# Steps of the last two block inverses put sooner in their slots, and the last output product split by columns, in an RWKV-7 chunk kernel with a SoLU layer

## The chip, the cores and the metric

The kernel runs on one core of one Trainium2 chip. The metric is device time in microseconds of one execution, as the median of several runs. One execution was also recorded by the hardware profiler; its times are given in microseconds from the start of its span.

TensorE is PE in the profile (PEld is its weight load), VectorE is DVE, ScalarE is ACT, GpSimd is POOL, SyncE is SP. A "q" behind a name (ACTq, SPq) means the issue of a transfer by that engine's queue.

## The reference

Two blocks follow one another, all in float32. The first is a recurrence with a decaying state for each of 4 batches and 8 heads (sequence 768, head size 40); the second is a layer with a SoLU activation and a layer norm on the 3072 tokens of 320 numbers that the first gives.

```python
for t in range(S):                                   # per batch and head, state is 40 x 40
    y[t]  = r[t] @ state
    Sa    = state @ a[t]
    state = state * w[t][None, :] - outer(Sa, b[t]) + outer(v[t], k[t])
x = y rearranged to (3072, 320)
h = x @ w_in                                         # 320 -> 1024
sm = exp(h - max(h)) / sum(exp(h - max(h)))
solu = h * sm
ln = (solu - mean(solu)) / sqrt(var(solu) + 1e-6) * g_ln
out = ln @ w_out                                     # 1024 -> 320
```

## The kernel before

The sequence is cut in chunks of 64 tokens. A unit of work, here called chunk i, is one such piece for a pair of batches with all 8 heads; there are N = 24 of them, two pairs of batches in turn, so chunks i and i + 2 belong to the same sequence. Inside a chunk the recurrence is written as matrix products, which need the inverse of a triangular 64 x 64 matrix for each head and batch. That inverse is put together from 32 x 32 blocks.

**The inverses.** The blocks of two chunks (GRP = 2) are inverted together by `invert`, a Python generator. VectorE works them out column by column: a *step* is one pair of instructions, a product (`prod`, L428) and a subtraction from `uu` (L430), and there are 30 steps for an inverse. All steps of one inverse depend on one another. The blocks come in by transfers issued on POOL (`blk<-nt_dram`, L412), from the matrices `nt` that earlier chunks wrote to memory (L401). With the last step two transfers are issued on SP (L436) that write the result to `uu_dram`; `bring` later reads it into `tu` and `uh` (L449, L451, also on SP). There are 12 inverses; the last two are numbered 10 (chunks 20 and 21) and 11 (chunks 22 and 23).

**The order of work.** All engines follow the order in which the program is written (`manual_schedule`). The main loop runs over i from -1 to 27 as a software pipeline: iteration i prepares chunk i + 5 (`front`, `norm`, AHEAD = 5), scores chunk i + 1, finishes the state of chunk i, and runs the second block for chunks i - 2 to i - 4 (`hidden`, `highest`, `exped`, `weighed`, `spreadof`, `folded`, `output`). Near the end the parts for chunks past 23 drop out. From i = 16 on there are no more loads of `w`; `norm` runs for the last time at i = 18 and `solved` at i = 23.

**The slots.** The steps of the inverse are dealt out by `some(n)` at four places of an iteration, called slots 0 to 3 here; how many a slot takes is in `shares`, or a default:

```python
pieces = shares.get(i, (0, 5, 4, 4) if i % GRP else (3, 5, 4, 5))
```

On VectorE the order within an iteration is: slot 0; the masks of `psi` and `lv` (L375) and the product `aT` (L366); slot 1; the *flip*, a 32 x 32 transpose of `tu` (L457); the row maximum `nmax` (L670); slot 2; the masks of `nt` and `lu` (L375); the product `e` (L684) and the statistics (L692 to L700); slot 3; the output `x` of the chunk (L619) and its state sum `tot` (L634). An inverse is begun in an even iteration, ahead of slot 3, but takes its first step only in the next iteration.

TensorE's order within an iteration is: `pu`, `ps`, `pst`, turned inputs `pa` and `pb`, two products into `h`, the first half of the output product `po`, `py` (which reads the flipped `tu`), `pnt`, `pl`, the second half of `po`, `pz`, `pyo` (which reads `lu`), `px`, more of `h` and `pyo`, the transposes `plnT`, then `pk`, `pv`, `pr`. The PSUM tiles `pu`, `ps`, `py`, `pnt`, `pl`, `pz`, `pyo` and `px` share two buffers (`ps1`, bufs = 2), so each waits until an earlier one has been read. While `norm` runs, `pz` takes over a buffer that the mask of `nt` reads, and `pyo` one that the mask of `lu` reads; from i = 19 on, without `pnt`, `pyo` still follows `lu`.

`xT` (L625, L626 on SP) takes `x` on to the second block; these transfers stand on SP ahead of the reads of the next iteration's `bring`.

**The output.** `output(i, 0)` does the first four of the eight products of chunk i with `w2` (width DM = 320) into one PSUM bank, `output(i, 1)` the last four; then ScalarE scales the bank into `osb` (L727) and issues its transfer to memory (L728). `osb` has a single buffer, so it can be written again only when the transfer before has ended. In the last iteration, i = 27, nothing but the output of chunk 23 is left. The lnT tile that it reads is copied by ScalarE in two halves (L713), four of the eight products from each.

Of the kernel before, what the change touches and what calls it, by code (L numbers as in the profile page):

```python
# [9 lines left out]
FP32 = mybir.dt.float32  # L10
# [3 lines left out]
AF = mybir.ActivationFunctionType  # L14
# [3 lines left out]
P = 128  # L18
C = 64
# [29 lines left out]
def kernel(  # L49
# [18 lines left out]
    nc = tc.nc  # L68
    B, H, S, D = r.shape
    DM = H * D  # L70
# [3 lines left out]
    N = NPAIR * NCH  # L74
    NF = DFF // P
# [5 lines left out]
    two = ctx.enter_context(tc.tile_pool(name="two", bufs=2))  # L81
# [14 lines left out]
    def c_(name):  # L96
        lo, hi = where[name]
        return cst[:, lo:hi]
# [20 lines left out]
    for x in ex_t:  # L119
# [10 lines left out]
                          in_=c_("eye_hi").unsqueeze(1).to_broadcast([P, 8, Q]))  # L130
    w_in = const.tile([P, 2 * NK - 1, DFF // 2], FP32, name="w_in")
    w2 = const.tile([P, NF, DM], FP32, name="w2")
# [6 lines left out]
    def bank(name):  # L139
        return ps3.tile([P, 512], FP32, tag="bank", name=name)  # L140
# [133 lines left out]
    def where_(i):  # L274
        return i % NPAIR, i // NPAIR
# [7 lines left out]
    def ok(i):  # L283
        return 0 <= i < N
# [430 lines left out]
    def output(i, x):  # L715
        if not ok(i):
            return
        d = st[i]
        bp, ci = where_(i)
        if x == 0:  # L720
            d["out"] = bank("po")
        for f in range(x * NF // 2, x * NF // 2 + NF // 2):
            nc.tensor.matmul(d["out"][:, 0:DM], lhsT=d["lnT"][:, f, :], rhs=w2[:, f, :], start=f == 0, stop=f == NF - 1)  # L723
        if x == 0:
            return
        osb = two.tile([P, DM], FP32, tag="osb", name="osb", bufs=1)
        nc.scalar.activation(out=osb, in_=d["out"][:, 0:DM], func=AF.Copy, scale=d["rs"])  # L727
        nc.scalar.dma_start(out=out.rearrange("(b s) n -> b s n", b=B)[2 * bp:2 * bp + 2, ci * C:ci * C + C], in_=osb)  # L728


    steps = []
# [79 lines left out]


    shares = {-1: (0, 2, 3, 9), 0: (4, 5, 3, 4), 1: (0, 6, 4, 5), 2: (4, 4, 3, 4), 3: (0, 5, 4, 4), 4: (6, 1, 4, 6)}
    narrowed = {-1: (0, 1, 0), 0: (0, 1, 1), 1: (1, 0, 2), 2: (0, 1, 2), 3: (1, 0, 1)}
    for i in range(-1, N + 3 + LAG):
        j, m = i + AHEAD, i - LAG
# [29 lines left out]
        left(i - 1)  # L846
        decay(j + 2)
        output(m - 3, 0)

        some(pieces[2])  # L850
# [12 lines left out]
        if i == 2 + LAG:  # L863
            mean = mean_of(4, 6, mean)
        output(m - 3, 1)

        close(i + 1)
# [48 lines left out]
```

## Time and profile before

| what | value |
|---|---|
| median of 3 runs | 621.12 us (618.76 to 623.91) |
| profiled execution, own time | 617.47 us |
| its span | 615.7 us |
| mean granted TensorE clock | 0.938 |
| TensorE busy | 547.3 us (89%) |
| VectorE busy | 448.7 us (73%) |
| ScalarE busy | 265.6 us (43%) |
| GpSimd busy | 257.7 us (42%) |
| start of `pu` in iterations 17, 18, 19, 20, 21 | 443.31, 464.27, 485.00, 505.16, 524.56 us |

A line of a timeline or group reads: start, length in us, engine, line of the program, operation, output <- inputs, partitions x elements, count, and in brackets how long the engine had stood still before it and what ended that. A line of the chain of waits has start, length and what ran; the chain is followed back from the last instruction to whatever released each one. The slices of the page cut the span in 40 equal parts, with the busy share in tenths (9 is 90% or more).

### The profile page before, as it was taken

Reading aid. Unit: us, or ns where it says so; the run is one execution under the profiler, and the core shown is the slowest. Engines: PE = TensorE matmul, PEld = TensorE weight load, DVE = VectorE, ACT = ScalarE, POOL = GpSimd, SP = SyncE. Lnnn points to the kernel's source line nnn. Section 1 sums busy time; section 2 is a strip of 40 time slices with the busy share of each in tenths; the row PEclk is TensorE's granted clock in tenths of the full one; section 3 lists DMA queues with packets and bytes.
Section 4 is the critical chain, followed back from the end, with each engine's and each line's share of the span. In section 5 each row is a group of like instructions: output and inputs, shape, how many; then the busy total and the mean of one; then the engine's idle time right before and its main releaser. Section 6 shows DMA issues by size and latency. Waiting matters only on the chain.

```text
span 615.7 us, 26656 instructions
## 1 busy us (share of the span) xinstructions
PE 547.3 (89%) x11453; PEld 397.4 (65%) x11453; DVE 448.7 (73%) x1262; ACT 265.6 (43%) x548; POOL 257.7 (42%) x424
## 2 busy tenths in 40 slices
PE   4555587689899999999999999999999999999994
PEld 3334476566576777777777677777777676676652
DVE  4797978979968869868868868688698688443431
ACT  4434455454443544454454445444433343342221
POOL 3462272472452472473365355534624631322200
PEclk9666767789999999999999999999999999999998
DMA  8986895664445454564565574564532612310100
GB/s 166 156 157 132 176 176 107 139 137 84 82 105 98 94 118 94 97 118 99 94 122 97 95 127 97 111 110 82 109 56 53 122 44 44 65 35 26 28 19 21
DMA packets 213901, 59.93 MB, mean 97 GB/s; under 512 B 199120, under 2 KB 208952, under 8 KB 213784
## 3 DMA queue, kind: packets, MB, share of 16 engines
q1 hardware_dynamic: 195512, 33.78, 32.5%
q0 software_dynamic: 11568, 19.78, 13.9%
q10 hardware_dynamic: 6704, 4.67, 2.7%
q8 instruction: 90, 1.47, 1.0%
q14 instruction: 27, 0.22, 0.1%
HBM read 40.10 MB, written 13.37 MB: 87 GB/s over the span
## 4 chain that ended last, share of the span: by engine, by line
PE 71%; DVE 15%; DMA 4%; issue 3%; ACT 3%; SPq 1%; POOL 1%; ACTq 0%; DVEq 0%; POOLq 0%
PE po L723 16%; PE h L257 15%; PE pyo L257 7%; DVE prod L428 4%; DVE uu L430 4%; PE pu L257 4%; PE plnT L712 4%; PE ps L257 3%; PE px L257 3%; PE py L257 2%; PE pl L257 2%; PE pz L257 2%; PE pst L505 2%; PE pr L342 1%; PE pei L342 1%
## 5 line engine op out<-in xcount | busy, mean ns | idle before, releaser
L257 PE MATMUL h<-w_in,xT 128*128 128x512 f32 (+1 forms) x288 | 123.0, 610 | 0.0
L723 PE MATMUL po<-w,lnT 128*128 128x320 f32 x384 | 112.7, 438 | 0.5 <-ACT lnT L713 0.5
L430 DVE TENSOR_TENSOR uu<-uu,prod 128x30 f32<-128x30 f32 (+4 forms) x360 | 102.1, 284 | 12.4
L428 DVE TENSOR_TENSOR prod<-blk,uu 128x30 f32<-128x30 f32 (+4 forms) x360 | 97.6, 271 | 9.6
L723 PEld LDWEIGHTS po<-w,lnT 128*128 128x128 f32 x384 | 71.0, 190 | 32.6 <-issue 4.1
L401 POOL DMA_DIRECT2D nt_dram<-nt x20 | 18.9, 943 | 120.0 <-DVE nt L375 98.5
L375 DVE TENSOR_TENSOR psi<-ps,cst 128x512 f32<-128x512 f32 x24 | 16.6, 690 | 66.6 <-PE ps L257 66.6
L701 POOL TENSOR_TENSOR rs<-c,mhalf 128x1 f32<-128x1 f32 x24 | 13.5, 561 | 112.1 <-DVE c L700 103.2
L650 POOL DMA_DIRECT2D xT<-x x96 | 48.7, 512 | 0.0
L257 PEld LDWEIGHTS h<-w_in,xT 128*128 128x128 f32 (+1 forms) x288 | 37.4, 189 | 9.2 <-issue 8.1
L670 DVE TENSOR_REDUCE nmax<-h 128x1 f32<-128x1024 f32 x24 | 28.6, 1193 | 18.6 <-PE h L257 18.6
L412 POOL DMA_DIRECT2D blk<-nt_dram x46 | 36.6, 802 | 10.8 <-issue 6.8
L257 PE MATMUL pyo<-lv,kb 64*64 64x104 f32 x768 | 37.8, 266 | 2.2
L257 PEld LDWEIGHTS pyo<-lv,kb 64*64 64x64 f32 x768 | 23.9, 140 | 20.9 <-issue 20.8
L638 POOL TENSOR_TENSOR st<-tot,ex 104x160 f32<-104x160 f32 x44 | 21.8, 512 | 36.6 <-DVE tot L634 23.5
L257 PE MATMUL pyo<-lu,kb 64*64 64x104 f32 x768 | 36.7, 258 | 0.0
L469 ACT ACTIVATE wy<-py,cst 128x256 f32<-128x256 f32 x24 | 11.4, 473 | 56.2 <-PE py L257 56.2
L280 POOL DMA_DIRECT2D raw_r<-in_r_dram x48 | 33.9, 709 | 0.0
L727 ACT ACTIVATE osb<-po,rs 128x320 f32<-128x320 f32 x24 | 12.7, 527 | 48.5 <-PE po L723 32.9
L554 ACT COPY x<-px 128x320 f32<-128x320 f32 x24 | 10.2, 425 | 54.1 <-PE px L257 54.0
L678 ACT ACTIVATE e<-h,nmax 128x1024 f32<-128x1024 f32 x24 | 26.6, 1108 | 14.3 <-DVE nmax L670 14.3
L684 DVE TENSOR_TENSOR e<-h,e 128x1024 f32<-128x1024 f32 x24 | 29.2, 1217 | 4.6 <-ACT e L678 4.6
(128 smaller groups left out, 1162.6 us busy)
## 6 DMA issues: line engine op xcount, KB each, us to landing
blk<-nt_dram POOLq DMA_DIRECT2D x46, 128.0 KB, 4.4
nt_dram<-nt POOLq DMA_DIRECT2D x20, 256.0 KB, 3.5
raw_w<-in_w_dram SPq DMA_DIRECT2D x48, 80.0 KB
a<-in_a_dram SPq DMA_DIRECT2D x48, 80.0 KB
raw_r<-in_r_dram POOLq DMA_DIRECT2D x48, 80.0 KB, 3.1
lv<-in_v_dram SPq DMA_DIRECT2D x48, 80.0 KB
out_dram<-osb ACTq DMA_DIRECT2D x24, 160.0 KB
raw_b<-in_b_dram SPq DMA_DIRECT2D x44, 80.0 KB
```

Source lines behind the costliest of these rows:

```text
L257: nc.tensor.matmul(o, lhsT=lhsT, rhs=rhs, start=start, stop=stop, skip_group_check=True)
L280: queue.dma_start(out=x[half(p), :, 0:D], in_=ap[2 * bp + p, :, ci * C:(ci + 1) * C, :].rearrange("h t d -> t h d"))
L412: queue.dma_start(out=nb[home:home + Q], in_=blocks[n][:, Q * e:Q * e + Q, Q * e:Q * e + Q])
L428: nc.vector.tensor_tensor(out=t, in0=nb[:, j:j + 1, j + 1:Q].to_broadcast([P, n_c, m]), in1=u[:, 0:n_c, j:j + 1].to_broadcast([P, n_c, m]) ...
L430: nc.vector.tensor_tensor(out=u[:, 0:n_c, j + 1:Q], in0=u[:, 0:n_c, j + 1:Q], in1=t, op=ALU.subtract)
L638: nc.gpsimd.tensor_tensor(out=to3(old), in0=to3(tot[0:W2]), in1=ex[:, :, 2 * q:2 * q + 2, C:].to_broadcast([W2, 2, 2, D]), op=ALU.mult)
L650: nc.gpsimd.dma_start(out=xT[to:to + Q, 2], in_=x[at + P - 3 * D:at + D, 2])
L670: nc.vector.tensor_reduce(out=nmax, in_=d["h"], axis=AX.X, op=ALU.max, negate=True)
L678: nc.scalar.activation(out=e, in_=d["h"], func=AF.Exp, bias=d["nmax"], accum_out=d["esum"])
L684: nc.vector.tensor_tensor(out=d["e"], in0=d["h"], in1=d["e"], op=ALU.mult)
L712: nc.tensor.transpose(out=t[:, j * P:(j + 1) * P], in_=d["e"][:, f * P:(f + 1) * P], identity=ident)
L723: nc.tensor.matmul(d["out"][:, 0:DM], lhsT=d["lnT"][:, f, :], rhs=w2[:, f, :], start=f == 0, stop=f == NF - 1)
```

## The change

Two edits. The first gives iterations 17 to 20 their own entries in `shares`, so that the 30 steps of inverse 10 (iterations 17 and 18) and of inverse 11 (19 and 20) are dealt out in other slots. The counts before, by the default, are 0,5,4,4 in 17 and 19 and 3,5,4,5 in 18 and 20. The entries of 18 and 20 add up to more than is left of the inverse; what is left is taken, so slot 3 of iteration 18 and slots 2 and 3 of iteration 20 stay empty, and slot 1 of iteration 20 takes five.

The second concerns chunk 23 alone. Its `output(23, 0)` issues nothing, and `output(23, 1)` makes all eight products for the left 160 columns, scales and sends them, and then the same for the right 160 columns in another PSUM bank. The two halves of `osb` are written and sent separately.

```diff
+        to = out.rearrange("(b s) n -> b s n", b=B)[2 * bp:2 * bp + 2, ci * C:ci * C + C]
+        osb = two.tile([P, DM], FP32, tag="osb", name="osb", bufs=1) if x else None
+
+        if i == N - 1:
+            for lo in (0, DM // 2) if x else ():
+                part = slice(lo, lo + DM // 2)
+                t = d["out"] if lo == 0 else bank("po")
+                for f in range(NF):
+                    nc.tensor.matmul(t[:, part], lhsT=d["lnT"][:, f, :], rhs=w2[:, f, part], start=f == 0, stop=f == NF - 1)
+                nc.scalar.activation(out=osb[:, part], in_=t[:, part], func=AF.Copy, scale=d["rs"])
+                nc.scalar.dma_start(out=to[:, :, part], in_=osb[:, part])
+            return
...
-        osb = two.tile([P, DM], FP32, tag="osb", name="osb", bufs=1)
         nc.scalar.activation(out=osb, in_=d["out"][:, 0:DM], func=AF.Copy, scale=d["rs"])
-        nc.scalar.dma_start(out=out.rearrange("(b s) n -> b s n", b=B)[2 * bp:2 * bp + 2, ci * C:ci * C + C], in_=osb)
+        nc.scalar.dma_start(out=to, in_=osb)
...
     shares = {-1: (0, 2, 3, 9), 0: (4, 5, 3, 4), 1: (0, 6, 4, 5), 2: (4, 4, 3, 4), 3: (0, 5, 4, 4), 4: (6, 1, 4, 6)}
+    shares.update({17: (0, 6, 5, 6), 18: (5, 6, 2, 4), 19: (0, 7, 6, 6), 20: (6, 6, 4, 4)})
```

## The prediction

> **What bounds the kernel now.** I read the page's busy line and slices first, then the chain that ended last, then the timelines of TensorE and VectorE through iterations 17 to 20 (443 to 524 us, the only ones whose step counts change), then the end. Lines from all of them, in that order:
>
> ```profile
> PE 547.3 (89%) x11453; PEld 397.4 (65%) x11453; DVE 448.7 (73%) x1262; ACT 265.6 (43%) x548; POOL 257.7 (42%) x424
> PE   4555587689899999999999999999999999999994
> DVE  4797978979968869868868868688698688443431
> ...
> 487.93 4.10 DMA tu<-uu_dram
> 492.12 0.46 DVE tu L457
> 492.71 0.67 PE py L257 x32
> ...
> 471.76 0.67 PE L257 MATMUL py<-tu,nt 64*64 64x32 f32 x32
> 492.71 0.67 PE L257 MATMUL py<-tu,nt 64*64 64x32 f32 x32 [1.18 <-DVE tu L457]
> 496.64 0.67 PE L257 MATMUL pyo<-rT,s 40*64 40x64 f32 x32
> 512.13 0.67 PE L257 MATMUL py<-tu,nt 64*64 64x32 f32 x32 [0.43 <-DVE tu L457]
> ...
> 466.43 0.69 DVE L375 TENSOR_TENSOR psi<-ps,cst 128x512 f32<-128x512 f32 x1 [2.35 <-PE ps L257]
> 471.26 0.44 DVE L457 STREAM_TRANSPOSE tu<-tu 128x256 f32<-128x256 f32 x1
> 492.12 0.45 DVE L457 STREAM_TRANSPOSE tu<-tu 128x256 f32<-128x256 f32 x1 [0.79 <-DMA tu<-uu_dram]
> 495.78 0.68 DVE L375 TENSOR_TENSOR lu<-pl,cst 128x512 f32<-128x512 f32 x1
> 511.55 0.44 DVE L457 STREAM_TRANSPOSE tu<-tu 128x256 f32<-128x256 f32 x1
> ...
> 608.31 0.53 ACT L727 ACTIVATE osb<-po,rs 128x320 f32<-128x320 f32 x1 [4.23 <-PE po L723]
> 608.87 0.53 ACTq L728 DMA_DIRECT2D out_dram<-osb  x1
> ...
> DMA  0000001111110111110111111111100000000001
> GB/s 0 0 0 0 0 15 29 15 44 59 15 51 7 51 37 37 37 15 37 44 59 44 44 59 44 59 44 44 51 0 0 0 0 0 0 0 0 0 0 47
> ```
>
> TensorE is full (9 in every slice from the middle to the last) and mostly hands over to itself. In the four iterations it stands still for only 1.18 and 0.43 us, both times ahead of `py`, for the flip (L457). The first of these waits has a transfer behind it: the tenth inverse's write (5.29 us in the chain) and read (4.10 us). VectorE is not the bound by its sum, but two things in its queue release TensorE in every iteration: the flip, which `py` waits for, and the masks at L375, which free the PSUM buffers of `pz` and `pyo`. At iteration 18 the flip ends (471.26 + 0.44 = 471.70) just as TensorE arrives; at 19 the mask of `lu` ends at 496.46 and `pyo` starts at 496.64. There is next to no slack in front of either. The last two lines are 609 to 616 us in 0.175 us slices: the last output drains from 609.9 to 614.0 us at a tenth of the DMA engines.
>
> [...] The output is 2 x 64 x 320, [...] with a busy share of 0.13 to 0.14 (2 of 16 is 0.125). [...] Here a 1.7 us wait of `pk` for `lnT` leaves it at 1.00; this decides a rival below.
>
> **The change, first part: the steps.** It adds and removes no step. One step is a pair L428, L430 of 0.45 to 0.65 us from start to start (447.82 to 448.27 for the first; 458.71 to 459.34 for the eleventh). An iteration has four slots: 0 ahead of the masks of `psi`, 1 ahead of the flip, 2 ahead of the masks of `nt` and `lu`, 3 ahead of `x`. Counts before are 0,5,4,4 / 3,5,4,5 / 0,5,4,4 / 3,5,4,5 for iterations 17 to 20. After, they are 0,6,5,6 / 5,6,2,0 / 0,7,6,6 / 6,5,0,0, since each inverse has 30. So every flip gets more steps in front of it. I carry the delay S of TensorE through, with 0.58 us from a flip's start to `py` (492.12 to 492.71; 511.55 to 512.13) and 0.14 us from a mask's end to the matmul.
>
> Iteration 17. Slot 1 has one step more (0.52): flip at 450.67, `py` at 451.25 for 451.09. Slot 2 then holds steps 7 to 11, 2.9 us for 2.2: mask of `nt` from 455.04 to 455.72, of `lu` to 456.32. `pz` wants the buffer of `nt` and `pyo` that of `lu`; `pyo` starts at 456.46 for 455.82. S = 0.64. Slot 3 is six steps, 4.1 us; `x` and `tot` end near 464.7, before `ps` (465.23 + 0.64) needs their buffer.
>
> Iteration 18. Slot 0, five steps, 3.06 us: 464.64 to 467.70, while `psi` could start at 466.43 + 0.64 = 467.07. The masks and `aT` take 1.81, slot 1 is six steps, 3.06: flip at 472.57, `py` at 473.15 for 471.76. S = 1.39. Slots 2 and 3 are nearly empty, and VectorE catches up; nothing on TensorE waits for that.
>
> Iteration 19. The tenth inverse is done before 475.1 instead of 481.5; its last step issues the two `uu_dram` writes on SP, which stands idle there (its next are the `xT` transfers), so they hold up nobody, and its read, behind the four `xT` transfers on SP, lands near 490.2, and the transfer no longer holds the flip. But `psi` starts at 487.16 + 1.39 = 488.55, the new inverse's steps at 490.31, and seven of them are 3.42: flip at 493.73, `py` at 494.31 for 492.71. The wait of 1.18 us is not gained: what is late next is VectorE's own queue. S = 1.60. Slot 2 is six steps, 3.56 us for 2.2: `lu` from 498.77 to 499.45, `pyo` at 499.59 for 496.64. S = 2.95. This is the largest single term, 1.35.
>
> Iteration 20. Slot 3 of 19 and `x`, `tot` run to 507.84, slot 0 to 511.35 (`psi` could start at 507.32 + 2.95 = 510.27), then 1.20, then five steps of 2.2: flip at 514.75, `py` at 515.33 for 512.13. S = 3.20. SP's queue moves too: `xT` follows `x`, which is 4.5 us later, so the read of the inverse for chunk 21 is issued near 510.4 instead of 505.86 and lands near 514.8 by the 4.4 us from issue to landing of iteration 19 (487.56 to 492.03). That is level with the flip: 0.1 more. After that TensorE runs back to back, and no wait was there to be removed: S stays 3.3. Bounds: 2.3, if the 0.2 us stretches of steps beside POOL's work (463.16 against 462.69) and half the mask terms fall away, and 4.6, if the landing takes the 5.7 us that iteration 20 allows (505.86 to 511.55).
>
> **Second part: the last output.** Before, 16 matmul records of 320 columns, 0.269 us apart (8 in 2.15). After, 32 of 160 columns; no row has that form. If they cost by columns, 0.134 each and 4.3 in all, the same; transposes of 128 columns with a weight load each run at 0.109 (4 in 0.44), so the loads fit. Bounds: -0.2 and +1.0; I take 0. The left half is ready near 606.1, but `osb` has one buffer and must wait for the transfer of output 22 (L728 issued at 602.44, drained by 607.5). So left `osb` is at about 607.6 (0.40 us for 160 columns, from 527 ns for 320 and 1108 for 1024), its issue at 608.0; right `osb` 608.6, issue 609.0, 0.15 after the old one at 608.87. First bytes come 1.03 after an issue: 609.06 instead of 609.9. In the packet records 1280 bytes take 55 ns, 1024 take 46, 512 take 27, so 640 about 32, or 28.5 from start to start where 1280 have 52. Each of the two engines then has 128 packets, 3.65, and some 0.7 of slow first packets as before (64 x 0.052 = 3.3 of 4.1 us): end at 613.4 against 614.0. Gain 0.5; bounds -0.4 (slow first packets twice) and +1.9 (if `osb` had not to wait).
>
> **Sum.** +3.3 - 0.5 = +2.8 us on a span of 615.7, whose own time is 617.47: 618.5 and 620.3. The profiled execution was 3.65 under the median of the runs shown, so against 621.12 the forecast is 623.9, 0.5% slower. About 1% is what a measurement of this kernel can tell from no change.
>
> **Rivals.**
> (a) The forecast, 623.9: 0.60.
> (b) The earlier inverse does what an earlier inverse can: both waits (1.18 + 0.43) go and the end gains 0.5, -2.1: 619.0. For it: the wait's chain is the transfer. Against: seven steps now stand between mask and flip. 0.12.
> (c) The delays stay only at the flips, since the masks' buffers are freed in another order than I read, S about 1.9, and the end gains 1.0: +0.9, 622.0. 0.18.
> (d) The other side: SP at iteration 20. If the late `x` pushes the reads of `tu` and `uh` so that they collide, and `tu` lands 3.5 us later than I have it, each microsecond past 514.75 goes straight onto `py`: +6.3, 627.4. It decides from a landing later than about 515. For it: in-order issue behind `xT`. Against: iteration 20 before bounds the time to landing at 5.7 us, and that gives only +1.2. A throttled clock would do the same[...]. 0.10.
> That the change does nothing is no rival: the counts alter the order of VectorE's stream.
>
> Range: (a) with its bounds is 623.9 - 1.9 to + 1.5; (b) and (d) lie outside, and three runs scattered by 5 us. 619.8 to 628.0 holds 8 in 10. Faster by over 1% needs -6.2 and no case has it: 0.03 for scatter. Slower by over 1% is (d) and the top of (a): 0.09. Within 1%: 0.88.
>
> **What would show it.** `py` of iterations 18, 19, 20 starting 1.4, 1.6 and 3.2 later than before, with waits for the flip of about 0.8, 1.4 and 0.7 us; `pyo` at 19 waiting over 1 us for `lu`; no transfer behind the flip at 19; `osb` at the end waiting for the transfer of output 22. A `py` of 19 that comes earlier than before proves me wrong, as does a drain of the last output over 0.5 us shorter.

## The result, and the profile after

The changed kernel takes 624.73 us (median of 22 runs, 621.98 to 630.0) against 620.98 us (22 runs, 617.76 to 624.86): a ratio of 1.0063, 95% interval 1.0045 to 1.0081. By this ratio it is 3.9 us more (2.8 to 5.0). The forecast was 623.9 us, 2.8 us more, which is the lower end of that interval. The profiled execution has a span of 623.0 us for 615.7.

First TensorE's waits from 150 us on, before and then after: who waited for whom, us in total, times, longest.

```profile
PE pk L342 <- ACT lnT L713: 1.7, 1, 1.7
PE py L257 <- DVE tu L457: 1.6, 2, 1.2
PE ps L257 <- issue: 1.5, 2, 0.8
...
PE ps L257 <- issue: 3.0, 3, 1.3
PE py L257 <- DVE tu L457: 2.8, 3, 1.4
PE po L730 <- ACT lnT L713: 0.5, 1, 0.5
PE pk L342 <- ACT lnT L713: 0.5, 1, 0.5
PE pz L257 <- DVE nt L375: 0.3, 1, 0.3
```

`py` waits 2.8 us for the flip instead of 1.6, and `pz` now waits for the mask of `nt`. "issue" is a standstill to which the view gives no releaser; 0.5 of the 3.0 us lie in the four iterations and come back below. The wait of `pk` lies near 156 us, far ahead of the change. The timeline of TensorE and VectorE after, in iterations 17 to 20:

```profile
454.17 0.67 PE L257 MATMUL py<-tu,nt 64*64 64x32 f32 x32
458.77 0.67 PE L257 MATMUL pz<-uh,wy 64*64 64x32 f32 x32 [0.29 <-DVE nt L375]
476.07 0.67 PE L257 MATMUL py<-tu,nt 64*64 64x32 f32 x32 [0.90 <-DVE tu L457]
491.55 0.58 PE L257 MATMUL ps<-rT,vT 40*64 40x64 f32 x24 [0.50 <-issue]
498.00 0.67 PE L257 MATMUL py<-tu,nt 64*64 64x32 f32 x32 [1.42 <-DVE tu L457]
499.09 4.00 PE L735 MATMUL po<-w,lnT 128*128 128x320 f32 x8
503.57 0.67 PE L257 MATMUL pyo<-rT,s 40*64 40x64 f32 x32
519.00 0.67 PE L257 MATMUL py<-tu,nt 64*64 64x32 f32 x32 [0.44 <-DVE tu L457]
...
492.20 0.69 DVE L375 TENSOR_TENSOR psi<-ps,cst 128x512 f32<-128x512 f32 x1 [6.04 <-PE ps L257]
497.41 0.44 DVE L457 STREAM_TRANSPOSE tu<-tu 128x256 f32<-128x256 f32 x1
502.46 0.69 DVE L375 TENSOR_TENSOR lu<-pl,cst 128x512 f32<-128x512 f32 x1
```

The second half of `po` at 19 in the kernel before:

```profile
493.81 2.42 PE L723 MATMUL po<-w,lnT 128*128 128x320 f32 x8
```

At 18 `py` now waits 0.90 us. At 19 the bracket behind the flip (497.41) has gone: no transfer holds it, it stands in its own queue, and `py` waits 1.42 us for it. The second half of `po` at 19 takes 4.00 us where before it took 2.42; that is the granted clock (the share of its full speed that TensorE was given), which was 0.50 from 500 to 502 us, see below.

From the starts of `pu` (iterations 17 to 21: 446.29, 467.75, 489.31, 512.02, 531.44 us) the 7.3 us of span divide as follows: 2.98 lie before `pu` of 17, where the two programs are the same, so that is a difference between two executions; 3.90 in the four iterations (+0.50, +0.83, +2.55, +0.02); 0.11 from there to the last `po`, where the programs are again the same; and 0.33 from the last `po` to the end. The stretches in which the programs differ thus hold about 4.2 us, of which 0.73 turns out below to be a standstill that is not the change's.

The end: the last `po` before; then after; and then the transfer view after from 615 to 624 us, in slices of 0.225 us:

```profile
603.65 4.57 PE L723 MATMUL po<-w,lnT 128*128 128x320 f32 x16 [0.53 <-ACT lnT L713]
...
609.43 0.53 ACTq L739 DMA_DIRECT2D out_dram<-osb  x1
610.64 4.61 PE L730 MATMUL po<-w,lnT 128*128 128x160 f32 x32 [0.53 <-ACT lnT L713]
615.11 0.39 ACT L731 ACTIVATE osb<-po,rs 128x160 f32<-128x160 f32 x1 [4.03 <-DMA out_dram<-osb]
615.53 0.53 ACTq L732 DMA_DIRECT2D out_dram<-osb  x1
616.11 0.39 ACT L731 ACTIVATE osb<-po,rs 128x160 f32<-128x160 f32 x1 [0.60 <-ACT osb L731]
616.53 0.52 ACTq L732 DMA_DIRECT2D out_dram<-osb  x1
...
GB/s 0 0 0 0 0 0 0 17 34 46 40 23 20 20 46 46 46 40 46 46 46 46 46 46 46 34 0 0 0 0 0 0 0 0 0 36 0 0 0 0
```

The 32 short matmuls take 4.61 us where 16 long ones took 4.57: here the split costs TensorE 0.04 us. But the left `osb` waits 4.03 us, until 5.68 us after the issue of output 22, and both halves then go out in one stretch from 616.7 to 620.8 us, at no more than 46 GB/s.

### The profile page after: what moved, and what is told of

Read it like the earlier page. It is cut to its first block, busy times and chain, and to the rows that moved or that the text cites. A ratio compares the mean times of both kernels' runs of the same rounds, so it can differ in the third digit from the quotient of the medians.

```text
span 623.0 us, 26692 instructions
## 1 busy us (share of the span) xinstructions
PE 557.2 (89%) x11469; PEld 406.2 (65%) x11469; DVE 450.2 (72%) x1262; ACT 266.2 (43%) x549; POOL 257.7 (41%) x424
## 4 chain that ended last, share of the span: by engine, by line
PE 65%; DVE 22%; DMA 4%; ACT 4%; issue 3%; POOL 1%; SPq 0%; ACTq 0%; DVEq 0%; POOLq 0%
PE po L735 14%; PE h L257 14%; PE pyo L257 6%; DVE prod L428 6%; DVE uu L430 6%; PE plnT L712 3%; PE pu L257 3%; PE px L257 3%; PE ps L257 3%; PE py L257 2%; PE pl L257 2%; PE pz L257 2%; PE pst L505 1%; DMA raw_b<-in_b_dram 1%; PE pcum L325 1%
## 5 line engine op out<-in xcount | busy, mean ns | idle before, releaser
L735 PE MATMUL po<-w,lnT 128*128 128x320 f32 x368 | 109.7, 443 | 0.0
L735 PEld LDWEIGHTS po<-w,lnT 128*128 128x128 f32 x368 | 68.7, 191 | 31.3 <-issue 4.6
L554 ACT COPY x<-px 128x320 f32<-128x320 f32 x24 | 10.2, 426 | 55.3 <-PE px L257 55.1
```

## The experiments

All ratios are against the kernel before, run beside them, with a 95% interval.

**The two edits apart.** Steps alone:

```diff
     shares = {-1: (0, 2, 3, 9), 0: (4, 5, 3, 4), 1: (0, 6, 4, 5), 2: (4, 4, 3, 4), 3: (0, 5, 4, 4), 4: (6, 1, 4, 6)}
+    shares.update({17: (0, 6, 5, 6), 18: (5, 6, 2, 4), 19: (0, 7, 6, 6), 20: (6, 6, 4, 4)})
```

> Only the step counts of iterations 17 to 20 are changed; the last output is as before. Theory (VectorE's queue: more steps ahead of the flips and of the mask of lu): nearly the whole cost is here, +3.5 to +4.0 us, ratio 1.0055 to 1.0065, with TensorE waiting for the flip at 18 and 19 and pyo of 19 late by another 1.3 us or more after py. Rival (the cost sits at the end, or in clock drops and stalls of TensorE that one execution happened to have): within 1.5 us of before, ratio under 1.0025.

Measured: ratio 1.0056 (1.0036 to 1.0076), 3.5 us more. The output alone (the first two parts of the diff above, without the `shares` line):

> Only the last output is changed (two halves of its columns); the step counts are as before. Theory (the left osb waits for the transfer of output 22, so that the right half is issued 0.7 us later than the whole was): +0.3 us, ratio 0.9990 to 1.0020, left osb starting 5.6 to 5.7 us after the issue of output 22. The forecast's own figure was -0.5 us. Rival (the two halves overlap and shorten the end as meant): -1 to -2 us, ratio 0.9970 to 0.9985.

Measured: 0.9996 (0.9979 to 1.0013). The left `osb` starts at 616.40, 5.66 us after the issue of output 22 at 610.74. So the cost is in the steps, and for the split of the last output no effect is measured.

The steps alone show the wait that the clock hid in the changed kernel (TensorE's timeline):

```profile
475.19 0.67 PE L257 MATMUL py<-tu,nt 64*64 64x32 f32 x32 [0.90 <-DVE tu L457]
497.50 0.67 PE L257 MATMUL py<-tu,nt 64*64 64x32 f32 x32 [1.42 <-DVE tu L457]
502.69 0.69 PE L257 MATMUL pyo<-rT,s 40*64 40x64 f32 x32 [1.08 <-DVE lu L375]
518.49 0.67 PE L257 MATMUL py<-tu,nt 64*64 64x32 f32 x32 [0.88 <-DVE tu L457]
```

**The two inverses apart.** Only 17 and 18:

```diff
+    shares.update({17: (0, 6, 5, 6), 18: (5, 6, 2, 4)})
```

> Only iterations 17 and 18 have the new counts; 19 and 20 and the last output are as before. Theory: +1.3 us at py of 18, of which 0.8 us is given back at 19, because the tenth inverse is now there early and the flip of 19 waits for five steps only, not for a transfer: in all +0.5 us, ratio 1.0000 to 1.0020. Rival (delays add up and nothing is given back): +1.3 to +1.5 us, ratio 1.0025.

Measured: 1.0018 (1.0001 to 1.0034), which allows both. The trace, `py` of 18 and 19:

```profile
476.00 0.67 PE L257 MATMUL py<-tu,nt 64*64 64x32 f32 x32 [0.89 <-DVE tu L457]
497.19 0.67 PE L257 MATMUL py<-tu,nt 64*64 64x32 f32 x32 [0.29 <-DVE tu L457]
```

The wait at 19 falls from 1.18 to 0.29 us. That alone does not show that the earlier inverse gave it back: this profile also has a standstill of TensorE in iteration 19 (0.89 us), which puts `psi`, the five steps and the flip off. The batch version below has the old counts and a standstill too (1.16 us), and the same 0.29:

```profile
497.52 0.67 PE L257 MATMUL py<-tu,nt 64*64 64x32 f32 x32 [0.29 <-DVE tu L457]
```

What the earlier inverse did is seen on SP. The read of `tu` for chunk 20, before and with the new counts of 17 and 18:

```profile
487.56 1.84 SPq L449 DMA_DIRECT2D tu<-uu_dram  x2
488.64 2.29 SPq L449 DMA_DIRECT2D tu<-uu_dram  x2
```

Before, it is issued 2.56 us after `pu` of 19 (485.00), now 0.60 us ahead of it (489.24). With the 4.4 us to landing of the kernel before, it would land near 493.0, and the flip starts at 496.60; an estimate, which leaves the transfer 3.6 us to spare. So the transfer no longer holds the flip; how much of the wait goes by this alone is not shown. Only 19 and 20:

```diff
+    shares.update({19: (0, 7, 6, 6), 20: (6, 6, 4, 4)})
```

> Only iterations 19 and 20 have the new counts; 17 and 18 and the last output are as before. Theory: seven steps fit almost behind the transfer's wait, so py of 19 is 0.2 us late; the mask of lu after six steps makes it 1.6 at pyo; 1.9 us at py of 20: in all +1.9 us, ratio 1.0020 to 1.0040. Rival (only the flips count, masks do not gate TensorE): +0.2 to +0.7 us, ratio under 1.0015.

Measured: 1.0031 (1.0013 to 1.0050), 1.9 us more; `py` of 19 waits 1.42 us for the flip, `pyo` 1.08 us for the mask of `lu`, `py` of 20 0.88 us for the flip. The rival, by which the flips alone count, expected under 1.0015 and is weakened by the time and refuted by the wait of `pyo`.

**Flip and mask of iteration 19 apart.** One execution of each kernel, both with the changed counts of 17, 18 and 20:

```diff
-    19: (0, 7, 6, 6)
+    19: (0, 7, 4, 6)        # first kernel: seven ahead of the flip, four ahead of the mask
+    19: (0, 5, 6, 6)        # second kernel: five ahead of the flip, six ahead of the mask
```

> As the changed steps, last output as before, but iteration 19 has (0,7,4,6): seven steps ahead of the flip, four instead of six ahead of the mask of lu. Theory: py of 19 late as in the steps alone (a wait for the flip of about 1.4 us), but pyo following pz without a wait. Rival (masks never gate TensorE; the flips alone do): the same picture, so it tells only together with its twin.

> As the changed steps, last output as before, but iteration 19 has (0,5,6,6): five steps ahead of the flip as before, six ahead of the mask of lu. Theory: the wait for the flip of 19 falls to 0.3 to 0.5 us, and pyo waits about 1.1 us for the mask of lu. Rival (masks never gate): no wait at pyo.

Second kernel, TensorE's timeline:

```profile
501.90 0.67 PE L257 MATMUL py<-tu,nt 64*64 64x32 f32 x32 [0.29 <-DVE tu L457]
506.95 0.69 PE L257 MATMUL pyo<-rT,s 40*64 40x64 f32 x32 [0.94 <-DVE lu L375]
```

Five steps leave a wait of 0.29 us at the flip, and six in slot 2 make `pyo` wait 0.94 us. So slots 1 and 2 each have a reader of their own on TensorE. The two steps fewer at 19 came back in slot 1 of iteration 20, where six stood ahead of the flip and `py` waited 1.73 us. The first kernel waited 1.42 us at the flip and not at `pyo`, as expected, but its clock fell to a half there too (0.50 from 500 to 502 us) and brought `pz` 1.7 us late, so that the mask had the time anyway: its second half is not a clean test. The times of these single executions, 624.5 and 628.9 us for 620.2 before, tell nothing, since the 57 executions of the kernel before in the first group of experiments range from 616.8 to 625.8.

**The wait of the left half taken away.** On the kernel before, with the two halves:

```diff
-        osb = two.tile([P, DM], FP32, tag="osb", name="osb", bufs=1) if x else None
+        osb = (two.tile([P, DM], FP32, tag="osb2", name="osb2", bufs=1) if i == N - 1 else
+               two.tile([P, DM], FP32, tag="osb", name="osb", bufs=1)) if x else None
```

> Only the last output is changed: two halves of its columns as in the change, and osb of chunk 23 has a buffer of its own, so that the left half does not wait for the transfer of output 22. Step counts as before. Theory (that wait is what cost the halves their use): left osb about 2.5 us after the start of po instead of 4.5, drain of both halves ended some 1.8 us sooner than before, ratio about 0.997 (-1.8 us). Rival (two transfers on the same two engines are bound by their packets whenever they start): no gain, within 0.5 us.

Measured: 0.9965 (0.9946 to 0.9984), 2.2 us less. In the trace the left half starts when its matmuls are done, and from the last `po` to the end it is 10.27 us (608.63 to 618.9) instead of 12.03, 1.76 less:

```profile
608.63 4.61 PE L731 MATMUL po<-w,lnT 128*128 128x160 f32 x32 [0.53 <-ACT lnT L713]
611.17 0.39 ACT L732 ACTIVATE osb<-po,rs 128x160 f32<-128x160 f32 x1 [2.10 <-PE po L731]
613.28 0.39 ACT L732 ACTIVATE osb<-po,rs 128x160 f32<-128x160 f32 x1 [1.72 <-PE po L731]
```

**The number of engines.** Full width, but the last transfer cut by batch, so that two transfers of 64 x 320 take the place of one of 2 x 64 x 320. In the kernel before, that one has a busy share of 0.12 to 0.14 of the 16 engines in the windows from 610 to 614 us, about two of them:

```diff
+        to = out.rearrange("(b s) n -> b s n", b=B)
+        if i == N - 1:
+            for p, queue in enumerate((nc.scalar, nc.sync)):
+                queue.dma_start(out=to[2 * bp + p, ci * C:ci * C + C], in_=osb[half(p)])
+            return
```

> The last output in full width as before, but its transfer is cut by batch, 64 rows of 320 each, one issued on ACT and one on SP; step counts as before. Theory (the output 2 x 64 x 320 ran on two engines [...]): the drain of 4.1 us shrinks to under 1 us, -3.0 us, ratio about 0.995. Rival (the end is set by a fixed time from the last issue, not by the packets): within 0.5 us of before.

Measured: 0.9957 (0.9939 to 0.9975), 2.7 us less. The transfer view from 608 to 619 us, slices of 0.275 us, holds output 22 as it was and then output 23:

```profile
DMA  0001111111011111100000000059800000000000
GB/s 0 0 9 28 37 37 37 33 37 37 14 47 51 51 47 51 47 33 0 0 0 0 0 0 0 0 126 200 266 5 0 0 0 0 0 30 0 0 0 0
```

Output 22, uncut, runs at about 40 GB/s with a busy share of a tenth for 16 slices (4.4 us). Output 23, the same 160 KB, is through in some 3 slices (0.8 us) at up to 266 GB/s, with a busy share of 5 to 9 tenths. From the last `po` to the end it is 9.26 us (608.84 to 618.1) for 12.03. The edit changes two things, the engines of a transfer and the queues that issue it; the busy share shows the first, and what the second queue adds was not tried.

**Steps where nobody waits for them.** The tenth inverse done 1.8 us sooner, but no slot 1 or 2 fuller than before:

```diff
+    shares.update({17: (0, 5, 4, 6), 18: (5, 5, 4, 1), 19: (0, 3, 4, 6), 20: (4, 4, 4, 5)})
```

> Step counts (0,5,4,6), (5,5,4,1), (0,3,4,6), (4,4,4,5) for iterations 17 to 20: the tenth inverse ends about 1.8 us sooner, but no more steps than before stand ahead of any flip or mask; last output as before. Theory: both waits for the flip (1.18 and 0.43 us) go, -1.6 us, ratio 0.997 to 0.998. Rival (the idle time only moves on to the next wait): no gain, ratio 0.999 to 1.001.

Measured: 0.9989 (0.9962 to 1.0016), 0.7 us less, which is not told from no change and lies between the two theories. The trace has no wait for a flip left between 430 and 545 us:

```profile
PE ps L257 <- issue: 0.9, 1, 0.9
```

Its iterations 18, 19 and 20 last 20.58, 20.03 and 18.91 us for 20.73, 20.16 and 19.40, 0.77 us less in all, although 19 holds that standstill of 0.9 us, which the profile of before does not have. Both together:

> The step counts of the free-slots version and the last transfer cut by batch together. Theory: the two gains add, since one lies in iterations 19 and 20 and the other after the last matmul: -4.6 us, ratio 0.991 to 0.994. Rival (one of them is hidden): -3 us or less.

Measured: 616.4 us, ratio 0.9924 (0.9895 to 0.9953), 4.7 us less than before. This version is faster than both kernels. That the steps add to the batch cut is seen in its iterations 18 to 20 (20.59, 20.02 and 18.91 us) and not in the times, since its interval overlaps that of the batch cut alone (0.9939 to 0.9975).

## Why the prediction was right, point by point

**The steps: right, in size and place.** For each start, the time from `pu` of 17 less the same in the kernel before:

| S, us | forecast | after | steps alone | steps alone, less 1.12 from 19 on |
|---|---|---|---|---|
| `pyo` of 17 | 0.64 | 0.57 | 0.56 | 0.56 |
| `py` of 18 | 1.39 | 1.33 | 1.32 | 1.32 |
| `py` of 19 | 1.60 | 2.31 | 2.68 | 1.56 |
| `pyo` of 19 | 2.95 | 3.95 | 3.94 | 2.82 |
| `py` of 20 | 3.20 | 3.89 | 4.25 | 3.13 |

The excess at 19 is a standstill of TensorE inside `ps`, after 8 of its records `ps<-rT,vT`, for "issue". It puts `psi` off by 0.73 us in the changed kernel and 1.12 in the steps alone (`psi` starts 2.16 us after `pu` of 19 before, 2.89 and 3.28 there). It is not the change's: with the old steps the kernel with only the output changed has it at the same place (1.44 us) and so has the batch version (1.2), and the free slots have it too (0.9). Ten of the twelve profiles show it; those of the kernel before and of the one with the free buffer, both with the old steps, do not at this place. How often each kernel has it over many executions is not known. The records of transfers in the traces show what goes with it: in the ten profiles a transfer of 16 KB on the instruction queue (q8) lands 0.8 to 1.8 us after the start of `pu` of 19, and TensorE goes on 1.3 to 1.7 us after that landing (in the changed kernel it lands at 490.13, and TensorE goes on at 491.55); in the other two that transfer had landed 2.3 us ahead of `pu`. Whether TensorE waits for it no experiment tried. With the standstill taken off, the forecast's sum for the steps, 3.3 us, holds to 0.2. What the forecast did not see is that the change also takes away the cover. In the batch version, which has the old steps, the standstill puts `psi` off by 1.39 us, but iteration 19 is only 0.50 longer than before, since the wait for the flip shrinks from 1.18 to 0.29; behind seven steps nothing is left to shrink. That may be why the runs, at 3.9 us, lie above the forecast, whose 2.8 is at the edge of their interval. This last link is read from single profiles and was not tried by itself.

In the changed kernel's profile the sum closes: 3.2 us for the steps, 0.7 for the standstill and 0.3 for the end make the 4.2 of the stretches that differ, where the forecast has 3.3, nothing and -0.5. The total was right because its largest term was; no two errors cancelled.

**The wait with the transfer behind it: right.** It was forecast not to be gained, with VectorE's own queue late next, and the changed kernel shows it: no transfer in front of the flip, which starts (497.41) 0.18 us after the last instruction of the steps ahead of it (497.23), and 1.42 us of waiting. Rival (b) would need no more than five steps there. The kernel with only 17 and 18 changed has them, and its read is out 3.2 us sooner against `pu` of 19; how much that gives back stays open, since its standstill shortens the same wait. Rival (c), masks that do not gate, fell with the waits of `pyo` (1.08 and 0.94 us). Rival (d), a late landing of `tu` at 20, did not come: the flip there starts 0.09 us after the last instruction of the steps (518.42 and 518.33).

**The last output: the term was mis-sized.** Forecast -0.5 us, measured +0.33 in the trace and -0.2 (-1.3 to +0.8) in the runs of that edit alone. The mechanism, a left half that must wait for the transfer of output 22, was as forecast; the step of this term that failed is "drained by 607.5", which took the last packet for the end of the wait. The wait ends 5.68 us after the issue, not 5.16, and so the right half is issued 5.89 us after the start of `po`, 0.67 later than the whole was (5.22), not 0.15. The drain then ended some 10.2 us from the start of `po` for 10.4, read to a slice of about 0.2 us: 0.1 to 0.3 gained, not 0.5; and the end of the span comes some 2.2 us after it instead of 1.6, for a reason that stays open. The outer bound given for "if `osb` had not to wait", 1.9, is close to what the free buffer gave (1.76 in the trace).

**The clock: the argument failed.** The forecast set a throttled clock aside. What the profile of before shows for that is one gap, the 1.74 us for which `pk` waited at 156.40, with a granted clock of 1.00 from 154 to 162 us; how long a gap can be without a drop it does not show. Windows of the changed kernel (start and end, length, busy us of PE, PEld, DVE, ACT and POOL with their counts, then granted clock, DMA share, GB/s):

```profile
496.00:498.00 2.00, 0.58 (x4) 0.10 (x2) 1.83 (x8) 0.00 (x0) 0.00 (x0) 1.00 0.00 0
498.00:500.00 2.00, 2.00 (x67) 1.77 (x68) 1.90 (x5) 1.28 (x2) 0.00 (x0) 0.94 0.00 0
500.00:502.00 2.00, 2.00 (x5) 1.20 (x5) 1.76 (x8) 0.29 (x2) 0.00 (x0) 0.50 0.03 8
502.00:504.00 2.00, 2.00 (x63) 1.14 (x65) 1.97 (x4) 0.53 (x1) 0.00 (x0) 0.71 0.00 0
```

A gap of 1.42 us was followed by half the clock for some 3.4 us (what the last three windows lack of full clock is 1.7 us). So a gap shorter than the 1.74 us that left the clock alone was followed by a drop. Here it cost little: the mask of `lu` ends at 503.15, and in the steps alone `pyo`, which waits for that mask, starts 0.05 us after its end (502.69 and 502.64; the forecast took 0.14); at 503.57 it started some 0.4 us later than that (an estimate from these). With the old steps, where no such wait stood behind it, a drop cost more: in the kernel with only the output changed the standstill of 1.44 us in `ps`, which ended at 493.98, was followed by

```profile
494.00:496.00 2.00, 2.00 (x29) 1.55 (x30) 1.37 (x3) 0.46 (x1) 1.33 (x3) 0.66 0.29 60
496.00:498.00 2.00, 2.00 (x4) 0.80 (x3) 1.72 (x9) 0.12 (x1) 0.34 (x1) 0.50 0.34 56
```

and iteration 19 lasted 22.27 us for 20.16, where the batch version's 1.16 us, without a drop, made it 20.66. A gap of this size does not decide it alone: 16 of 21 were followed by no drop, see the end.

## What to carry to other kernels

Work that is put sooner in an engine's order must be counted against what stands behind it there: here slots 1 and 2 each had a reader on the bounding engine, and 1 to 2 steps too many ahead of it cost more than the wait that the earlier result was to remove. Fill the slots that nobody reads soon, and free the ones ahead of the hand-over; here that took 0.77 us off three iterations of the trace, too little for the times of that version alone to show. Before the end of a kernel is split for overlap, look at what the first part waits for (here a single buffer) and at how many engines the transfer keeps busy (here a tenth of them): cutting it by batch, on two queues, with 5 to 9 tenths busy, brought the end a further 1.0 us forward in the trace (9.26 us from the last `po` for 10.27), with no wait to mind. The times of these two versions do not tell them apart.

## What the runs showed of the hardware that was not expected

- From 150 us on, TensorE has 21 gaps of 1.4 us or more in the twelve profiles. Five were followed within 2 us by half the clock for about 3.4 us: 1.42 (after), 1.44 (output only), 1.42 (seven and four steps at 19), 1.42 and 1.70 (near 275 us, in the version with both gains and in the one with five and six steps at 19). The other 16, up to 1.75 us, were not. No smaller gap was. What decides between them stays open.
- TensorE stands still for 0.5 to 1.4 us at one place of `ps` in iteration 19 in ten of twelve profiles, and for 0.65 to 1.75 us at two earlier places (near 187 and 405 us) in all twelve, the kernel before too. At 19 it goes on 1.3 to 1.7 us after a transfer of the instruction queue has landed; whether it waits for that was not tried.
- An output of 160 KB took 4.1 us as one transfer of 2 x 64 x 320 (before: busy share 0.12 to 0.14), and under 1.1 us as two transfers of 64 x 320 (batch version: 5 to 9 tenths). In the changed kernel's end the packets of 640 bytes start 28 ns apart on an engine, half of the 52 ns of 1280 bytes (medians of the packet records, counting two engines).
